# Attention two units at a time over one ring of score banks, and two weight tiles loaded later in the experts

## The chip, the cores and the metric

One Trainium2 chip, one core. The metric is the device time of one execution in microseconds (us), taken as the median of the runs shown. The engines are named as the profile names them: PE (TensorE matmul), PEld (its weight load), DVE (VectorE), ACT (ScalarE), POOL (GpSimd), SP (SyncE, which here only issues DMAs).

## The reference, cut to what matters

```python
def reference(**kwargs):
    attn_out = _attn_ref(q, k, v, n_global=8, n_local=96)   # 2 x 8 heads x 768 x 64
    x = attn_out.transpose(0, 2, 1, 3).reshape(B, S, H * D) # 2 x 768 x 512
    x = _moe_ref(x, w_gate, w_local, w1, w2)                # 8 experts, one per token
    return _moe2_ref(x, w_theta, w_tok_r, w_tok_i, w_ch)

# attention: banded + first keys, a linear bias per head, softmax, times v
scores = q @ k.T / sqrt(64) + bias;  scores = where(keep, scores, -1e9)
a = exp(scores - max) / (sum + 1e-9);  attn_out = a @ v
# experts: per token one expert e (a sequential choice), p[e] * (relu(x @ w1[e]) @ w2[e])
# last part: theta = x @ w_theta; y = w_tok_r @ (x cos theta) + w_tok_i @ (x sin theta)
#            u = x + y; out = u + relu(u @ w_ch)
```

## The kernel before, in words

Everything is float32 at the interface. Where precision allows no single pass, an operand is split into a high and a low part and three products are taken. The program is written out in Python; each engine takes its instructions in the order in which the program issues them, and semaphores are set by the framework, which also guards PSUM by whole banks. So the order of the calls is the schedule.

There are three stages: attention with the routing of tokens to experts, the experts, and the last part (theta, token mixing, channel product).

**Attention.** A unit is one block of 128 queries of one batch and one pair of heads: 12 blocks (`BLOCKS`, alternating over the two batches) times 4 pairs, 48 units. The blocks 0 and 1 see 128 keys, the others 256 (the last 96 before the block, the first 32, the block's own 128). A unit goes through these steps:

- `u_qk` (L572): scores, PE. Each of the two heads uses 64 rows of the array (L583, three products of high and low parts: 6 matmuls, two at a time side by side; L587 for the first two blocks).
- `u_soft` (L592), once per head: DVE adds the bias and takes the minimum (L605), ACT takes the exponential with its sum (L615).
- `u_tr` (L631): 4 full-array transposes on PE (L638); `u_cp` (L641): ACT copies them from PSUM to SBUF (L647; for a few early units DVE, L645).
- `u_pv` (L650): times v, 8 matmuls on PE with 64 output columns each (L662), two at a time side by side.

When the 4 units of a block are done, `blk_evac` (ACT, L674), `blk_rinv`, the logits (`lg`, `lc`, `lt`, `ld`: L223, L227, L230, L235), `blk_tr` (L679) and `blk_store` (L688, DMA `xd<-xt`) follow, and for every two blocks ten routing stages (`ch` to `tk`).

The loop `for step in range(TAIL0)` (L899) takes one unit per step: scores of unit `step`, some warm-up matmuls in the first 12 steps, v-product of unit `step-6`, softmax of unit `step-1`, a high/low split of a coming block's q or k (cast on ACT or DVE, rest on POOL), the late block and routing stages that are due in this step (a dictionary `later`), then transposes and copy of unit `step-4`. From unit 40 on the order is the hand-written string `TAIL`; it ends with a first expert tile computed ahead (`lead_*`: a gather of 128 rows, L750, and `lead_h`, `lead_y`).

PSUM in this stage: `pS` (scores: two buffers for each head, `s0` and `s1`), `pT` (2 buffers, shared by the transposes of probabilities, the transposed block `y`, the logits and the slot table), `pX` (v-product), `pM` (routing rows and warm-up).

**Experts.** Eight experts in order of size, each in 8 steps of 128 hidden columns, so `for u in range(64)` (L1524). Weights come in 512 KB pieces of two steps: `load_piece(n, (1,))` for w1 (ring of 3) and `(n, (2,))` for w2 (ring of 5), issued by SP in program order. The first ones are issued before the loop: piece 0 of w1, then the list `LOADS`. In step u: `mm1(u+2)` (L1404), `mm2(u)` (L1443, L1454), the split of w1 for u+3 (`split_w1`: ACT L1268, DVE L1269; a finished pair triggers the next w1 load), the split of w2 for u+1 (`split_w2`: ACT L1371, DVE L1372), `relu(u+2)`. In steps 2 and 3 ACT issues the first two loads of the matrices of the last part (`job_load`, L390, `jraw`); a background job (`job`, L395) works on them in between, first with an ACT instruction on the loaded data (L407). In step 1 two small stores of the token probabilities (`pd`, L1554) are issued.

**Last part.** Starts when the experts' rows are stored; its bulk is the token mixing on PE (L1712).

Of the kernel before, what the change touches and what calls it, by code (L numbers as in the profile page):

```python
# [9 lines left out]
F32 = mybir.dt.float32  # L10
# [7 lines left out]
PSUM = bass.MemoryType.PSUM  # L18
# [3 lines left out]
E, DM, FF = 8, 512, 1024  # L22
# [37 lines left out]
TAIL = """  # L60
pv34 yt7 sa39 tr36 cp36 ys7 qk40 pv35 ro3 sb39 tr37 ev8 sc3 cp37 sa40 tr38 cp38 qk41 sb40 oh3 ho3 pv36 lg8
sa41 lc8 sb41 qs11 fi ri8 pv37 po3 fi tr39 qk42 ks11 cp39 pv38 ri9 pl3 pv39 ev9 mk3 sa42 sb42 lt8 yt8 ld8 fi
# [19 lines left out]
W0, W1 = 8, 0  # L82
LOADS = ((1, 1), (0, 2), (2, 1), (1, 2), (2, 2), (3, 2), (4, 2))
PU = 1
# [18 lines left out]
def kernel(  # L103
# [339 lines left out]
    with ExitStack() as actx:  # L443
        ab = actx.enter_context(tc.tile_pool(name="ab", bufs=3, side="right"))
        ap = actx.enter_context(tc.tile_pool(name="ap", bufs=3, side="right"))
        pS = actx.enter_context(tc.tile_pool(name="pS", bufs=2, space=PSUM))
        pT = actx.enter_context(tc.tile_pool(name="pT", bufs=2, space=PSUM))
# [114 lines left out]

        SPLITS = {3: lambda: split_q(2), 4: lambda: split_k(2), 8: lambda: split_k(1)}

        WARM = dict.fromkeys(range(12), WPS) | {3: 6} | dict.fromkeys(range(4, 9), 2)

# [4 lines left out]

        def u_qk(u):  # L572
            n, j = units[u]
            sp = [pS.tile([128, 256], F32, tag=f"s{hh}", name=f"s{hh}") for hh in range(2)]
            cols = slice(j * 128, (j + 1) * 128)
            half = [slice(64 * hh, 64 * hh + 64) for hh in range(2)]
            b, t = divmod(n, NT)
            if t:
                kh, kl = [x[:, b, j, t * 160 - 96 : t * 160 + 160] for x in kparts]
                qh, ql = [w[:, BLOCKS.index(n) % 4, cols] for w in qparts]  # L580
                for i, (qa, ka) in enumerate(((qh, kh), (ql, kh), (qh, kl))):
                    for hh in range(2):
                        PE.matmul(sp[hh], lhsT=qa[half[hh]], rhs=ka[half[hh]], start=(i == 0), stop=(i == 2))  # L583
            else:
                q, k = packs[n]
                for hh in range(2):
                    PE.matmul(  # L587
                        sp[hh][:, 0:128], lhsT=q[half[hh], j], rhs=k[half[hh], j, 32:160], start=True, stop=True
                    )
            ust[u] = {"s": sp}  # L590

        def u_soft(u, hh):  # L592
            n, j = units[u]
            W = 256 if n % NT else 128
            bias = bias1 if n % NT else bias0
            if hh == 0:
                ust[u]["t"] = (
                    ap.tile([128, 2, 256], F32, tag="sm", name="sm"),
                    ap.tile([128, 2, 256], F32, tag="pr", name="pr", bufs=5),
                    ap.tile([128, 2], F32, tag="st", name="st", bufs=4),  # L600
                )
# [74 lines left out]
        def blk_tr(n):  # L676
            yp = yps[n] = pT.tile([128, 512], F32, tag="pt", name="y")
            for j in range(4):
                PE.transpose(yp[:, j * 128 : (j + 1) * 128], xTs[n][:, j], ident)  # L679
# [17 lines left out]
        def mps(own):  # L697
            return (pM if own else pT).tile([128, 512], F32, tag="m" if own else "pt", name="m")

# [42 lines left out]
        def lead_x():  # L742
# [5 lines left out]
            V.tensor_copy(head_i, idf)  # L748
            x = head["x"] = ap.tile([128, 2, 256], F32, tag="sm", name="x0")
            G.indirect_dma_start(  # L750
# [21 lines left out]
        def lead_tr():  # L772
            x = head["x"].rearrange("p a c -> p (a c)")
            tp = head["xp"] = pS.tile([128, 4, 128], F32, tag="s0", name="x0T")
            for j in range(4):
                PE.transpose(tp[:, j], x[:, j * 128 : (j + 1) * 128], ident)

        def lead_cp():
            xT = ap.tile([128, 2, 256], F32, tag="sm", name="x0T")
            head["xT"] = xT.rearrange("p a (b c) -> p (a b) c", b=2)  # L780
            A.activation(head["xT"], head.pop("xp"), AF.Copy)
            head["h"], head["hs"] = {}, {}

        def lead_h(f, c):
            if c == 0:
                head["h"][f] = pS.tile([128, 128], F32, tag="s1", name="h0")
            w = head["w"][f][:, 0].rearrange("p (a f) -> p a f", a=4)
            for j in (2 * c, 2 * c + 1):
                PE.matmul(head["h"][f], lhsT=w[:, j], rhs=head["xT"][:, j], start=(j == 0), stop=(j == 3))  # L789

        def lead_r(f):
            if f % 4 == 0:
                h = ap.tile([128, 2, 256], F32, tag="sm", name="h0")
                head["hs"][f // 4] = h.rearrange("p a (b c) -> p (a b) c", b=2)
            A.activation(head["hs"][f // 4][:, f % 4], head["h"].pop(f), AF.Relu)

        def lead_y(f, c):
            if f == 0 and c == 0:
                head["y"] = pS.tile([128, DM], F32, tag="s0", name="y0")
            o = slice(c * 256, (c + 1) * 256)  # L800
# [63 lines left out]

        later, pairs = {}, {}

# [31 lines left out]

        for step in range(TAIL0):  # L899
            n, j = units[step]  # L900
            i = step // 4 + 2
            if j == 0 and step and i < NB:
                load_qk(i)
                load_v(i)
            u_qk(step)
            warm(WARM.get(step, 0))
            u = step - 1
            if u == 2:
                mask1()
            if 0 <= u < 4:  # L910
                biases(0, u)
            if 5 <= u < 9:
                biases(1, u - 5)
            done = None
            if step >= 6:
                u_pv(step - 6)
                if units[step - 6][1] == 3:
                    done = units[step - 6][0]
            if u >= 0:
                u_soft(u, 0)  # L920
            if done is not None:
                blk_evac(done)
            if u >= 0:
                u_soft(u, 1)
            i = step // 4 + 1
            if step in SPLITS:
                SPLITS[step]()
            elif 2 < i < NB and step % 4 == 1:
                split_q(i)
            elif 2 < i < NB and step % 4 == 2:  # L930
                split_k(i)
            if done is not None:
                blk_rinv(done)
                st = blk_done(done)
                for lag, names in ((1, ("lg", "lc")), (2, ("lt", "ld"))):
                    for k in names:
                        after(step + lag, st[k])
                if done >= NT:
                    st = pairs[done % NT] = pair_stages(done % NT)
                    for lag, names in ((2, ("ch",)), (3, ("ro", "sc")), (4, ("oh", "ho")), (5, ("po", "pl", "mk")), (8, ("sl", "tk"))):  # L940
                        for k in names:
                            after(step + lag, st[k])
                after(step + 3, partial(blk_tr, done))
                after(step + 3, partial(blk_store, done))
            for fn in later.pop(step, []):
                fn()
            if step >= 4:
                u_tr(step - 4)
                u_cp(step - 4)
            if step == 20:  # L950
                scalars()
                window_flag()
            if step >= 16 and step % 2:
                fill()
        assert all(s < TAIL0 for s in later) or True

        ops = {}
        for u in range(NU):
# [5 lines left out]
            ops[f"pv{u}"] = partial(u_pv, u)  # L964
        blks = {}

# [325 lines left out]
    with ExitStack() as mctx:  # L1292
# [231 lines left out]
        for u in range(64):  # L1524
# [10 lines left out]
            if u in (2, 3):  # L1535
                job_load()
            mm1(u + 2)
            mm2(u)
# [422 lines left out]
```

## Time and profile before

| | us |
|---|---|
| median of 3 runs | 514.17 (513.6 to 516.56) |
| the profiled execution | 510.26 |
| its span, first to last instruction | 508.5 |
| PE busy in the span | 481.8 |
| DVE, ACT, POOL busy | 352.0, 267.6, 146.4 |

The span is cut into 40 slices of 12.7 us; a digit is the busy share of an engine in a slice in tenths. Attention takes the first 8 slices (to about 104 us), the work ahead on the first expert tile the next two, the experts follow up to two thirds of the row, and the last part is the rest. Busy time is a union: two matmuls side by side count once. The clock that PE was granted stands beside it in tenths of full speed.

### The profile page before, as it was taken

The page shows a single profiled execution, that of the slowest core. Times are in us where ns is not written, and L with a number is a line of the kernel's source. Part 1 is how long each engine was busy: PE and PEld are TensorE (multiplying, and loading weights), DVE is VectorE, ACT ScalarE, POOL GpSimd, SP SyncE. Part 2 cuts the span into 40 slices and gives each one's busy share as a digit, 9 for nine tenths or more (in the row PEclk, how much of TensorE's full clock was granted, in tenths as well). Part 3 has the DMA queues.
Part 4 walks back from the last instruction along what each step waited for, and adds up shares of the span by engine and source line. Part 5 has one row for each costly group of instructions (what it writes and reads, how often), then busy time and mean ns, then how long its engine had stood idle before and what let it go on. Part 6 is the DMA issues. An engine that isn't in the chain of part 4 may idle for free.

```text
span 508.5 us, 9738 instructions
## 1 busy us (share of the span) xinstructions
PE 481.8 (95%) x3416; PEld 393.2 (77%) x3417; DVE 352.0 (69%) x963; ACT 267.6 (53%) x647; POOL 146.4 (29%) x164
## 2 busy tenths in 40 slices
PE   8999999979849999999999989989999999999996
PEld 4577777658738889878888777868888888888886
DVE  6887777935637688876788989547787787571522
ACT  5787888651425566655556556446556365340300
POOL 6445753323203230302122011111534244250300
PEclk9999999999988999999999999999999999999999
DMA  8557565377977698777799984320132000000022
GB/s 282 166 150 233 175 219 190 144 246 246 306 191 241 190 334 294 238 249 245 232 321 340 339 295 163 131 105 0 36 112 62 22 21 22 0 1 31 32 105 83
DMA packets 53253, 86.34 MB, mean 170 GB/s; under 512 B 6512, under 2 KB 28784, under 8 KB 53200
## 3 DMA queue, kind: packets, MB, share of 16 engines
q1 hardware_dynamic: 44644, 64.82, 38.9%
q10 hardware_dynamic: 5804, 13.93, 8.2%
q0 software_dynamic: 2752, 6.93, 4.6%
q8 instruction: 28, 0.46, 0.4%
q14 instruction: 25, 0.20, 0.2%
HBM read 71.17 MB, written 14.49 MB: 168 GB/s over the span
## 4 chain that ended last, share of the span: by engine, by line
PE 72%; DMA 11%; DVE 9%; issue 3%; ACT 2%; POOL 1%; ACTq 0%; DVEq 0%; POOLq 0%
PE a L1712 20%; PE o L1443 7%; PE b L1749 7%; PE th L1636 6%; PE h L1404 6%; PE x L662 4%; DMA raw<-in_w_dram 4%; PE h L1388 4%; PE pt L638 3%; PE s L583 3%; DMA jraw<-in_w_tokT_dram 2%; DVE w2s L1372 2%; PE o L1454 2%; DMA jraw<-in_w_theta_dram 2%; PE h L789 2%
## 5 line engine op out<-in xcount | busy, mean ns | idle before, releaser
L1712 PE MATMUL a<-wtok,z 128*128 128x512 f32 x576 | 105.3, 341 | 0.0
L1712 PEld LDWEIGHTS a<-wtok,z 128*128 128x128 f32 x576 | 88.5, 188 | 13.1 <-ACT z L1687 0.3
L1443 PE MATMUL o<-w2s,hh 128*128 128x512 f32 x192 | 66.4, 421 | 2.8 <-DVE w2s L1372 1.6
L1404 PE MATMUL h<-xT,w1s 128*128 128x288 f32 (+3 forms) x384 | 54.7, 290 | 10.1 <-ACT w1s L1268 7.2
L1404 PEld LDWEIGHTS h<-xT,w1s 128*128 128x128 f32 x384 | 50.5, 193 | 14.4 <-ACT w1s L1268 7.9
L615 ACT ACTIVATE pr<-sm,st 128x256 f32<-128x256 f32 (+1 forms) x96 | 46.1, 483 | 11.6 <-DVE st L605 11.6
L1372 DVE TENSOR_TENSOR w2s<-raw,w2s 128x512 fp32r<-128x512 f32 x64 | 44.0, 688 | 5.3 <-ACT w2s L1371 2.7
L1388 PE MATMUL h<-xT,raw 128*128 128x192 f32 (+1 forms) x256 | 44.4, 316 | 1.0 <-issue 0.9
L1036 POOL DMA_INDIRECT xg<-xd,xidx x17 | 16.8, 990 | 96.8 <-PE tr L1243 90.9
L1388 PEld LDWEIGHTS h<-xT,raw 128*128 128x128 f32 x256 | 39.6, 189 | 5.2 <-issue 3.2
L1371 ACT ACTIVATE w2s<-raw 128x512 fp32r<-128x512 f32 x64 | 39.8, 623 | 4.3 <-DMA raw<-in_w_dram 2.0
L1443 PEld LDWEIGHTS o<-w2s,hh 128*128 128x128 f32 x192 | 33.0, 188 | 9.5 <-DVE w2s L1372 4.4
L1418 ACT ACTIVATE hh<-h 128x128 fp32r<-128x128 f32 (+3 forms) x64 | 20.4, 319 | 34.6 <-PE h L1404 18.8
L1443 PE MATMUL o<-w2s,hl 128*128 128x512 f32 x96 | 38.1, 397 | 0.0
L605 DVE CUSTOM_DVE_ANT_0 sm<-s,bias 128x256 f32<-128x256 f32 (+1 forms) x96 | 34.3, 392 | 0.2
L1668 POOL TENSOR_TENSOR si<-si,yg 128x512 f32<-128x512 f32 x10 | 13.4, 1344 | 60.7 <-ACT si L1661 51.4
L662 PE MATMUL x<-ps,vv 128*64 128x128 f32 x352 | 29.4, 286 | 0.3 <-ACT xT L674 0.2
L647 ACT ACTIVATE ps<-pt 128x512 f32<-128x512 f32 (+1 forms) x44 | 24.9, 567 | 8.1 <-PE pt L638 7.7
L638 PE MATMUL pt<-ident,pr 128*128 128x128 f32 x176 | 28.4, 281 | 0.4 <-ACT pr L615 0.3
L1757 DVE SCALAR_TENSOR_TENSOR ob<-b,xTf 128x512 f32<-128x512 f32 (+1 forms) x16 | 8.8, 557 | 27.6 <-PE b L1749 27.6
L1269 DVE TENSOR_TENSOR w1s<-raw,w1s 128x512 fp32r<-128x512 f32 x32 | 22.1, 689 | 8.1 <-ACT w1s L1268 7.4
L583 PE MATMUL s<-wtok,qp 64*128 64x256 f32 x240 | 25.2, 313 | 0.1
(264 smaller groups left out, 951.3 us busy)
## 6 DMA issues: line engine op xcount, KB each, us to landing
raw<-in_w_dram SPq DMA_DIRECT2D x64, 512.0 KB
qk<-in_pack_dram SPq DMA_DIRECT2D x11, 576.0 KB
jraw<-in_w_tokT_dram ACTq DMA_DIRECT2D x11, 512.0 KB
vv<-in_pack_dram SPq DMA_DIRECT2D x10, 512.0 KB
w<-in_w_dram SPq DMA_DIRECT2D x16, 256.0 KB
yd<-zero SPq DMA_DIRECT2D x13, 256.0 KB
xd<-xt SPq DMA_DIRECT2D x12, 256.0 KB
jraw<-in_w_tokT_dram ACTq DMA_DIRECT2D x10, 256.0 KB
```

The costliest lines, as they stand in the source:

```text
L583: PE.matmul(sp[hh], lhsT=qa[half[hh]], rhs=ka[half[hh]], start=(i == 0), stop=(i == 2))
L605: V.tensor_tensor_reduce(out=sm[:, hh, 0:W], in0=ust[u]["s"][hh][:, 0:W], in1=bias[:, 2 * j + hh], scale=-0.125, scalar=BIG, op0=ALU.add, ...
L615: A.activation(pr[:, hh, 0:W], sm[:, hh, 0:W], AF.Exp, bias=st[:, hh : hh + 1], scale=-1.0, accum_out=sums[n][:, 2 * j + hh : 2 * j + hh + 1],
L638: PE.transpose(pt[:, hh, c], pr[:, hh, c * 128 : (c + 1) * 128], ident)
L662: PE.matmul(xp[64 * hh : 64 * hh + 64, j], lhsT=vv[:, i, h * 64 : (h + 1) * 64], rhs=ps[:, hh, c], start=(c == 0), stop=(c == nch - 1),)
L1371: A.activation(h2, bb[:, o], AF.Copy)
L1372: V.tensor_tensor(l2, bb[:, o], f32(h2), op=ALU.subtract)
L1388: PE.matmul(hp[:, :N], lhsT=pieces[u // 2][1][:, j, o * 128 : (o + 1) * 128], rhs=x[:, j, :N], start=(j == 0), stop=(j == 3),)
L1404: PE.matmul(hp[:, :N], lhsT=wa[:, j], rhs=xa[:, j, :N], start=(k == 0), stop=(k == 11))
L1443: PE.matmul(out[:M], lhsT=ha[:, lo : lo + M], rhs=wa, start=(f == 0 and q == 0), stop=(f == 7 and q == 2),)
L1712: PE.matmul(acc[b][d][o], lhsT=za[:, d * 128 : (d + 1) * 128], rhs=wa[:, c, lo:hi], start=(t == 0 and n == 0 and (o == 0 or d % 2 == 0)), ...
L1749: PE.matmul(op[:, : hi - lo], lhsT=wa[:, d, e * 128 : (e + 1) * 128], rhs=ua[:, d, lo:hi], start=(n == 0), stop=(n == 11),)
```

## The change

Two independent parts.

First, the attention loop takes two units per step (`p`), `a = 2p` and `b = 2p+1`. Their scores share banks: one `[128, 512]` bank per head, unit a in columns 0 to 255, unit b in 256 to 511. `pS` becomes one ring of 4 banks (tag `s`), from which the transposed block `y`, the logits and the slot table also take a bank each (before: from `pT`); in the tail each unit takes two banks of this ring. The result of the first expert tile moves from `pS` to `pX`. Softmax of a pair follows its scores in the same step. Three SBUF rings grow by one buffer. The warm-up matmuls are dealt out anew (25 in place of 22), the splits of blocks 1 and 2 sit in steps 1 to 3 of the pairs, and the first line of `TAIL` is adapted.

Second, the w2 pieces 3 and 4 leave `LOADS` and are issued in steps 1 and 3 of the experts.

```diff
-LOADS = ((1, 1), (0, 2), (2, 1), (1, 2), (2, 2), (3, 2), (4, 2))
+LOADS = ((1, 1), (0, 2), (2, 1), (1, 2), (2, 2))
...
-        pS = actx.enter_context(tc.tile_pool(name="pS", bufs=2, space=PSUM))
+        pS = actx.enter_context(tc.tile_pool(name="pS", bufs=4, space=PSUM))
...
-        SPLITS = {3: lambda: split_q(2), 4: lambda: split_k(2), 8: lambda: split_k(1)}
-        WARM = dict.fromkeys(range(12), WPS) | {3: 6} | dict.fromkeys(range(4, 9), 2)
+        SPLITS = {1: lambda: split_q(2), 2: lambda: split_k(2), 3: lambda: split_k(1)}
+        WARM = dict(enumerate((2, 8, 6, 4, 3, 2)))
...
-        def u_qk(u):
+        def u_qk(u, with_last=False):
             n, j = units[u]
-            sp = [pS.tile([128, 256], F32, tag=f"s{hh}", name=f"s{hh}") for hh in range(2)]
+            if with_last:
+                sp = [x[:, 256:512] for x in ust[u - 1]["banks"]]
+            else:
+                banks = [pS.tile([128, 512], F32, tag="s", name=f"s{hh}") for hh in range(2)]
+                sp = [x[:, 0:256] for x in banks]
...
         def blk_tr(n):
-            yp = yps[n] = pT.tile([128, 512], F32, tag="pt", name="y")
+            yp = yps[n] = pS.tile([128, 512], F32, tag="s", name="y")
...
         def mps(own):
-            return (pM if own else pT).tile([128, 512], F32, tag="m" if own else "pt", name="m")
+            return (pM if own else pS).tile([128, 512], F32, tag="m" if own else "s", name="m")
...
-        for step in range(TAIL0):
...
+        for p in range(TAIL0 // 2):
+            a, b = 2 * p, 2 * p + 1
+            i = a // 4 + 2
+            if a % 4 == 0 and p and i < NB:
+                load_qk(i)
+                load_v(i)
+            u_qk(a)
+            u_qk(b, True)
+            warm(WARM.get(p, 0))
+            i = a // 4 + 1
+            if p in SPLITS:
+                SPLITS[p]()
+            elif 2 < i < NB:
+                (split_q if p % 2 else split_k)(i)
...
+            u_soft(a, 0)
+            u_soft(b, 0)
+            full_mode(p)
+            if p >= 2:
+                u_tr(a - 4)
+                u_cp(a - 4)
+                u_tr(b - 4)
+            u_soft(a, 1)
+            u_soft(b, 1)
+            if p >= 2:
+                u_cp(b - 4)
+            for fn in early.pop(p, []):
+                fn()
+            if p >= 3:
+                u_pv(a - 6)
+                u_pv(b - 6)
+                n, j = units[b - 6]
+                if j == 3:
+                    blk_evac(n)
+                    blk_rinv(n)
...
             if u in (2, 3):
                 job_load()
+            if u in (1, 3):
+                load_piece(3 + u // 2, (2,))
```

`full_mode(p)` runs the late block and routing stages that are due in step p (`lt`, `ld`, `yt`, `ys`, `ch` to `tk`); `early` holds the logits (`lg`, `lc`) of a block that was finished one step before.

## Rows read from the trace of the kernel before

**Rows 1.** The page: span, and PE busy in 40 slices (tenths).
```profile
span 508.5 us, 9738 instructions
...
PE   8999999979849999999999989989999999999996
```

**Rows 2.** Busy time by stretch; columns as the first line names them.
```profile
core 0: us, PE busy (x) PEld busy (x) DVE busy (x) ACT busy (x) POOL busy (x), PEclk, DMA share, GB/s
...
16.00:24.00 8.00, 7.95 (x70) 4.38 (x69) 7.64 (x29) 5.95 (x24) 4.36 (x3) 1.00 0.53 164
24.00:82.00 58.00, 57.85 (x633) 42.39 (x633) 44.85 (x220) 48.17 (x155) 30.89 (x30) 1.00 0.62 194
82.00:104.00 22.00, 20.75 (x240) 15.48 (x236) 19.42 (x95) 15.48 (x46) 7.22 (x10) 1.00 0.40 145
...
144.00:151.50 7.50, 0.25 (x2) 0.06 (x1) 0.51 (x2) 1.29 (x3) 0.00 (x0) 0.86 0.67 117
151.50:156.50 5.00, 4.88 (x16) 4.23 (x17) 4.97 (x11) 2.10 (x5) 0.00 (x0) 0.52 0.67 181
```

**Rows 3.** PE in order of time: start, us, what, count; one step of the loop.
```profile
62.43 0.66 PE L638 MATMUL pt<-ident,pr 128*128 128x128 f32 x4
63.02 0.62 PE L583 MATMUL s<-wtok,qp 64*128 64x256 f32 x6
63.57 0.66 PE L662 MATMUL x<-ps,vv 128*64 128x128 f32 x8
64.16 0.33 PE L230 MATMUL m<-ident,lT 128*128 128x128 f32 x1
```

**Rows 4.** PE in order of time, where two units' work stands together.
```profile
84.53 1.09 PE L638 MATMUL pt<-ident,pr 128*128 128x128 f32 x8
85.55 0.62 PE L583 MATMUL s<-wtok,qp 64*128 64x256 f32 x6
...
103.56 1.09 PE L662 MATMUL x<-ps,vv 128*64 128x128 f32 x16
104.59 0.33 PE L230 MATMUL m<-ident,lT 128*128 128x128 f32 x1
```

**Rows 5.** Line L583 from 24 to 82 us: matmul duration, least, median, most (ns).
```profile
L583 PE MATMUL s<-wtok,qp x164: 271/277/387, 23.9 to 80.1; 64*128 64x256 f32 x164
```

**Rows 6.** Chain of waits from 5 to 24 us: start, us, what.
```profile
22.31 1.57 POOL wtok L498
...
23.93 0.38 PE s L583
```

**Rows 7.** All engines in order of time in the tail; idle time before in brackets.
```profile
90.85 0.62 PE L583 MATMUL s<-wtok,qp 64*128 64x256 f32 x6
...
92.11 0.23 DVE L235 TENSOR_TENSOR lh<-m,sums 128x72 f32<-128x72 f32 x1
...
92.48 0.43 PE L223 MATMUL m<-xT,wg 128*32 128x128 f32 x8 [1.01 <-ACT pr L615]
```

**Rows 8.** Chain of waits over the whole span: two loads for the background job.
```profile
141.83 8.35 DMA jraw<-in_w_theta_dram
...
285.79 4.30 DMA jraw<-in_w_tokT_dram
```

**Rows 9.** PE in order of time at the start of the experts.
```profile
143.81 0.39 PE L1443 MATMUL o<-w2s,hl 128*128 128x512 f32 x1
151.44 3.73 PE L1404 MATMUL h<-xT,w1s 128*128 128x288 f32 x12 [7.25 <-ACT w1s L1268]
```

**Rows 10.** SP's queue: the loads of expert weights, merged.
```profile
129.38 4.44 SPq L1024 DMA_DIRECT2D raw<-in_w_dram  x4
134.07 3.51 SPq L1020 DMA_DIRECT2D raw<-in_w_dram  x2
```

**Rows 11.** DMA queues from 142 to 150 us (q1 is SP's, q10 ACT's).
```profile
q1 hardware_dynamic: 2540, 0.99, 48.8%
q10 hardware_dynamic: 144, 0.52, 16.9%
```

More of the change, by code (lines that the diff above doesn't have):

```diff
@@ L60 @@
 TAIL = """
-pv34 yt7 sa39 tr36 cp36 ys7 qk40 pv35 ro3 sb39 tr37 ev8 sc3 cp37 sa40 tr38 cp38 qk41 sb40 oh3 ho3 pv36 lg8
+pv34 lt7 ld7 yt7 tr36 cp36 ys7 sl2 tk2 ch3 qk40 pv35 ro3 tr37 ev8 sc3 cp37 sa40 tr38 cp38 qk41 sb40 oh3 ho3 pv36 lg8
 sa41 lc8 sb41 qs11 fi ri8 pv37 po3 fi tr39 qk42 ks11 cp39 pv38 ri9 pl3 pv39 ev9 mk3 sa42 sb42 lt8 yt8 ld8 fi
@@ L590, in u_qk @@
             ust[u] = {"s": sp}
+            if not with_last:
+                ust[u]["banks"] = banks
         def u_soft(u, hh):
@@ L597, in u_soft @@
                 ust[u]["t"] = (
-                    ap.tile([128, 2, 256], F32, tag="sm", name="sm"),
-                    ap.tile([128, 2, 256], F32, tag="pr", name="pr", bufs=5),
-                    ap.tile([128, 2], F32, tag="st", name="st", bufs=4),
+                    ap.tile([128, 2, 256], F32, tag="sm", name="sm", bufs=4),
+                    ap.tile([128, 2, 256], F32, tag="pr", name="pr", bufs=6),
+                    ap.tile([128, 2], F32, tag="st", name="st", bufs=5),
                 )
@@ L748, in lead_x @@
             V.tensor_copy(head_i, idf)
-            x = head["x"] = ap.tile([128, 2, 256], F32, tag="sm", name="x0")
+            x = head["x"] = ap.tile([128, 2, 256], F32, tag="sm", name="x0", bufs=4)
             G.indirect_dma_start(
@@ L773, in lead_tr @@
             x = head["x"].rearrange("p a c -> p (a c)")
-            tp = head["xp"] = pS.tile([128, 4, 128], F32, tag="s0", name="x0T")
+            tp = head["xp"] = pS.tile([128, 512], F32, tag="s", name="x0T").rearrange("p (j c) -> p j c", j=4)
             for j in range(4):
@@ L778, in lead_cp @@
         def lead_cp():
-            xT = ap.tile([128, 2, 256], F32, tag="sm", name="x0T")
+            xT = ap.tile([128, 2, 256], F32, tag="sm", name="x0T", bufs=4)
             head["xT"] = xT.rearrange("p a (b c) -> p (a b) c", b=2)
@@ L785, in lead_h @@
             if c == 0:
-                head["h"][f] = pS.tile([128, 128], F32, tag="s1", name="h0")
+                head["h"][f] = pS.tile([128, 512], F32, tag="s", name="h0")[:, 0:128]
             w = head["w"][f][:, 0].rearrange("p (a f) -> p a f", a=4)
@@ L792, in lead_r @@
             if f % 4 == 0:
-                h = ap.tile([128, 2, 256], F32, tag="sm", name="h0")
+                h = ap.tile([128, 2, 256], F32, tag="sm", name="h0", bufs=4)
                 head["hs"][f // 4] = h.rearrange("p a (b c) -> p (a b) c", b=2)
@@ L798, in lead_y @@
             if f == 0 and c == 0:
-                head["y"] = pS.tile([128, DM], F32, tag="s0", name="y0")
+                head["y"] = pX.tile([128, 4, 128], F32, tag="x", name="y0").rearrange("p j c -> p (j c)")
             o = slice(c * 256, (c + 1) * 256)
@@ L863, in experts_slots @@
             V.scalar_tensor_tensor(yidx, slotf[:, 0], 128.0, slotf[:, 1], op0=ALU.add, op1=ALU.add)
-        later, pairs = {}, {}
+        later, early, pairs = {}, {}, {}
         def after(step, fn):
@@ L897, in pair_stages, with full_mode @@
             return dict(zip(("ch", "ro", "sc", "oh", "ho", "po", "pl", "mk", "sl", "tk"), route_stages(t, mps, msb)))
-        for step in range(TAIL0):
-            n, j = units[step]
-            i = step // 4 + 2
-            if j == 0 and step and i < NB:
+        blks = {}
+        def full_mode(p):
+            for fn in later.pop(p, []):
+                fn()
[3 more added lines that the diff above has]
+            if a % 4 == 0 and p and i < NB:
@@ L903 @@
                 load_qk(i)
                 load_v(i)
[L905 to L944, printed above, removed]
@@ L945 @@
-            for fn in later.pop(step, []):
-                fn()
[L947 to L950, printed above, removed]
+            u_qk(a)
[6 more added lines that the diff above has]
+                (split_q if p % 2 else split_k)(i)
+            if p < 4:
+                t = p // 2
+                if p == 1:
+                    mask1()
+                for k in (2 * (p % 2), 2 * (p % 2) + 1):
+                    biases(t, k)
@@ new lines @@
+            u_soft(a, 0)
[10 more added lines that the diff above has]
+            for fn in early.pop(p, []):
+                fn()
+            if p >= 3:
[5 more added lines that the diff above has]
+                    blk_rinv(n)
+                    st = blks[n] = blk_done(n)
+                    early.setdefault(p + 1, []).extend(st[k] for k in ("lg", "lc"))
+                    after(p + 2, st["lt"])
+                    after(p + 2, st["ld"])
+                    after(p + 2, partial(blk_tr, n))
+                    after(p + 2, partial(blk_store, n))
+                    if n >= NT:
+                        st = pairs[n % NT] = pair_stages(n % NT)
+                        for lag, names in ((2, ("ch",)), (3, ("ro", "sc")), (4, ("oh", "ho")), (5, ("po", "pl", "mk")), (6, ("sl", "tk"))):
+                            for k in names:
+                                after(p + lag, st[k])
@@ L951 @@
+            if p == 10:
                 scalars()
                 window_flag()
-            if step >= 16 and step % 2:
+            if p >= 8:
                 fill()
-        assert all(s < TAIL0 for s in later) or True
         ops = {}
@@ L964 @@
             ops[f"pv{u}"] = partial(u_pv, u)
-        blks = {}
         def blk_op(i, k):
```

## The prediction

> **What bounds the kernel now.** I read the page's slices first: PE is at nine tenths in nearly every slice of a span of 508.5 us, with one hole of two slices [rows 1]. Then busy time by stretch. In the attention loop, 24 to 82 us, PE is busy 57.85 of 58 us while DVE has 44.85 and ACT 48.17; so PE is the bound there and the others have room. In the stretch before it DVE has 7.64 of 8 us, and in the tail, 82 to 104, DVE has 19.42 of 22: there DVE is as near to the bound as PE. From 144 to 151.5 PE does next to nothing, and afterwards its clock is granted at 0.52 for 5 us [rows 2].
>
> Busy is not the same as well used, so third the order of time on PE. One step of the loop: transposes start at 62.43, scores at 63.02, the v-product at 63.57, the next full-array work at 64.16. That is 0.59, 0.55 and 0.59 us, 1.73 us per unit [rows 3]. Where two units' transposes happen to stand together, eight take 1.02 us from 84.53 to the next kind, not 2 x 0.59; sixteen v-products take 1.03 us from 103.56 [rows 4]. So four more transposes cost 0.43 us and eight more v-matmuls 0.44: what is paid once per group, and not per matmul, is 0.16 and 0.15 us, the change from one shape of the array to another. Scores show the same inside a group: six matmuls in pairs take 0.62 us [rows 3] of which the last lasts 0.28 (the median), the first up to 0.39 [rows 5].
>
> Last the chain of waits. At the start of the experts ACT issues a background load at 141.83 that lands 8.35 us later [rows 8]; the split of w1 is queued behind its first use on ACT, and PE stands 7.25 us for it [rows 9].
>
> **The loop, 14 pairs (units 12 to 39).** It removes every second change of shape and adds no matmul. Per pair now 2 x 1.73 = 3.46 us. After: transposes 1.02, v-product 1.03 [rows 4], scores 0.55 plus three more pairs of matmuls. A further pair costs 0.11 us if it goes as the others do (0.43 / 4 and 0.44 / 4); from rows 3 and 5 alone it is at most (0.62 - 0.28) / 2 = 0.17. That gives 0.88 (at most 1.06), together 2.93 (3.11), a gain of 0.53 (0.35) per pair and of 7.4 us (4.9). I take the first, as it rests on two runs of the kind itself. The change from v-product straight to scores is not in the trace; either way I allow 0.1 us for it, 1.4 us in all.
>
> What hides the rest: block and routing stages are the same instructions as before. PE would need 57.85 / 14 - 0.53 = 3.60 us per pair, ACT has 48.17 / 14 = 3.44, DVE 44.85 / 14 = 3.20 [rows 2]. PE stays the bound, but ACT's cover shrinks from 0.69 to 0.16 us per pair, and order now matters. Two places where I see PE wait: in a step with a slot table the ring of four banks gives `y` the bank that `ld` on DVE must first read, about 0.5 us, twice in the loop; and ACT comes late at the second transposes' copy after an evacuation, some 0.4 us in sum. I give back 1.4 us: loop -6.0. If ACT became the bound outright it would still be 3.44 per pair; lost cover of 0.35 per pair is rival B.
>
> **The start, units 0 to 11.** DVE is nearly full (0.36 us idle in 16 to 24 [rows 2]), and the last wait before unit 12 is a split on POOL that ends at 23.88, just before its scores at 23.93 [rows 6]. The splits come one place earlier, three warm-ups are added on a PE that waits here anyway. I take -0.4, DVE's idle time. At best the split of 1.57 us leaves the path, -1.6; at worst the same on the other side, since the split of block 2's q now stands in front of four exponentials on ACT and waits there for its load: +1.6.
>
> **The tail.** The order stays, but scores, `y`, logits and the slot table share four banks. Counting allocations through the string, scores of unit 43 now need the bank that `ld8` reads; this read starts on DVE at 92.11, the scores went at 90.85. Before, PE stood 1.01 us at the logits right after that [rows 7], so this wait mostly takes that one's place; but units 44 and 45 and `y9` then each find a bank whose reader is one or two DVE instructions behind. About 0.7 us. The two waits of unit 47 lie beside the wait for a gather. Bounds 0, if DVE is that much earlier, and +2.5. If this part were serial it would be rival D.
>
> **The experts.** SP's bytes are the same, two loads move. Of the four w2 loads merged at 129.38 two leave; the two w1 loads at 134.07 [rows 10] move up. Piece 3 follows in step 1, behind the w1 load that waits for step 0, so before the background load at 141.83 again; piece 4 goes in step 3, behind ACT's split of step 2, so after it. From 142 to 150 SP's queue moves 0.99 MB and ACT's 0.52 [rows 11]: one piece of 0.52 MB less stands beside the background load. The least that such a load takes on the chain is 4.30 us [rows 8]; if the other 4.05 us are due to the 0.99 MB, 0.52 of them are worth 2.1 us. I take -2.1. Bounds 0 (it has its own 0.52 MB and two small stores beside it) and -4.05. ACT, SP and DVE issue nothing more than before; piece 4 is needed in step 7, some four steps after its issue. The granted clock has a mean of 0.86 over these 7.5 us [rows 2]: of its two levels, 2.4 and 1.2 GHz, that is the lower one for the last 2.1 us, so it fell some 5.2 us after the last matmul. A wait of 7.25 - 2.1 = 5.15 us lies right beside that; I take that it falls again, 0, and -2.3 if it does not (4.88 us of PE work at about half speed [rows 2]).
>
> **Sum.** -0.4 - 6.0 + 0.7 - 2.1 = -7.8 us. From 144 us on each stage waits for its own predecessors, so I carry it to the end whole. The profiled execution took 510.26 us, 3.91 below the median of 514.17; against the median the forecast is 506.4.
>
> **Rivals.**
> A, the forecast, 506.4.
>
> B, the shared bank: unit a's softmax may start only when unit b's scores are in the same bank, three pairs of matmuls later, 0.33 us. For it: ACT and DVE now start each pair behind PE, and before each head had a bank of its own. Against it: DVE's 3.20 us of 3.60. If all of it lies on the path, 14 x 0.33 = 4.6 us go: -3.2, 511.0. The Trainium skill, "PSUM — Partial Sum Buffer", section on bank collisions, has it as a rule that speaks against this change: guard PSUM "by **bank × quadrant** (by bank is the simple version), not by address"; no run here shows a read of one half while the other is written.
>
> C, the stall at 144 us goes further: the load lands as the fastest does, -4.05, and the clock stays, -2.3: -0.4 - 6.0 + 0.7 - 4.05 - 2.3 = -12.1, 502.1. For it: the DMA traffic there is what differs. Against: the load's own bytes, and a pause of 3 us remains.
>
> D, slower: scores of a pair wait for the last softmax of the pair before, through the ring. Then PE and DVE alternate: 0.88 + 0.28 + 3.20 = 4.36 us per pair against 57.85 / 14 = 4.13, +3.2; and in the tail, eight units, 0.55 + 0.28 + 19.42 / 8 = 3.26 each against 22 / 8 = 2.75, +4.1. With the start and the experts as above: -0.4 + 3.2 + 4.1 - 2.1 = +4.8, 519.0. It decides from the point where the bank that a pair's second head gets was last read by an instruction at the end of DVE's queue for the pair before. By my count of the ring that is so only in the two steps after a slot table, and in the tail for units 43, 44 and 47.
>
> E, the change does not do what it says: the time between groups is not the change of shape but a wait for the operands. Then the loop gives nothing: -1.8, 512.4. Against: rows 4 show the same operands' kinds without it.
>
> **Chances.** A 0.52, B 0.17, C 0.17, D 0.07, E 0.07. A measurement of this kernel tells about 0.5%, 2.6 us, from no change, so faster means under 511.6. A is that but for a fiftieth, C surely, B half: 0.76 faster. E, half of B and the rest of A: 0.17 the same. D: 0.07. The range from 500.5 (C with a good start) to 513.0 (E with a poor one) leaves out D and a little of either end.
>
> **What will show it.** In the changed profile: groups of 8 transposes, 12 scores, 16 v-products in the loop, the 12 scores in 0.88 us to the next kind, and the step for two units near 3.7 us; PE still full from 24 to about 76 us (if DVE or ACT ends its waits, B or D). Scores of unit 43 in the tail held by DVE. The background load landing some 6 us after its issue and PE's wait near 5 us, with the clock at half after it. I am wrong if the loop ends less than 3 us earlier, or if the tail grows by more than it gained.

## The result, and the profile after

The changed kernel took 508.06 us in the median of 4 runs, the kernel before 513.88: ratio 0.9871, 95% interval 0.9825 to 0.9918. The forecast was 506.4, range 500.5 to 513. The profiled execution took 507.36 us, before 510.26. On other chips the kernel before ran from 506.9 to 519.7 us; where the change ran again (e5), its median was 515.75 beside 513.46, and as five of its six runs lie over 1.5% above the sixth (505.83) and count as slow, there is no second ratio. Much of this spread goes with the clock: in a fit to the 125 runs that the comparisons use, with a level for each kernel, time falls 4.2 us per 0.01 of mean granted clock. At one clock the change stands 3.8 +- 1.8 us below before, its attention part alone (e1) 1.8 +- 1.4 below, its loads alone (e2) 0.3 +- 1.1 above (+- is two standard errors of the fit). With all 162 runs whose clock is on record in the fit, ten of them of the change, the change stands 1.8 +- 1.3 below. So a gain of 1.3% was not seen a second time.

So the total came out near the forecast. Its terms did not. The profile after, span and PE slices, to hold against [rows 1]:

```profile
span 505.6 us, 9746 instructions
...
PE   8888998989969999999999989899999999999996
```

Busy time by stretch, with the columns and four of the stretches of [rows 2]:

```profile
16.00:24.00 8.00, 7.79 (x78) 5.41 (x75) 5.18 (x24) 6.46 (x28) 4.13 (x4) 0.84 0.57 185
24.00:82.00 58.00, 51.64 (x617) 40.83 (x617) 43.22 (x215) 46.01 (x155) 29.81 (x30) 1.00 0.61 197
82.00:104.00 22.00, 20.82 (x225) 15.60 (x227) 18.59 (x89) 13.62 (x40) 6.66 (x9) 1.00 0.36 134
144.00:151.50 7.50, 3.47 (x13) 3.26 (x14) 4.21 (x9) 3.05 (x7) 0.00 (x0) 0.78 0.71 33
```

PE was full in the loop before, 57.85 of 58 us; now it does its work in fewer busy microseconds, 51.64, and stands for 6.4. The saving in array changes is there, and almost all of it has become waiting. The waits from 24 to 76 us (engine, line, whom it waited for: us in total, times, longest):

```profile
ACT pr L622 <- DVE xt L695: 12.0, 7, 2.1
...
DVE sm L612 <- PE s L588: 8.8, 7, 1.6
...
PE m L230 <- ACT lT L227: 2.1, 5, 0.7
...
PE pt L645 <- ACT ps L654: 1.7, 5, 0.4
...
PE m L334 <- POOL ohl L325: 0.9, 2, 0.7
```

Of ACT's waits in the kernel before, the same stretch, none is for `xt`:

```profile
ACT pr L615 <- DVE st L605: 5.0, 8, 1.1
ACT ps L647 <- PE pt L638: 4.0, 11, 0.6
```

One pair of the changed loop, all engines in order of time (start, us, engine, line, what; idle time before in brackets):

```profile
63.84 0.98 PE L588 MATMUL s<-wtok,qp 64*128 64x256 f32 x12
...
64.96 0.42 DVE L612 CUSTOM_DVE_ANT_0 sm<-s,bias 128x256 f32<-128x256 f32 x1 [1.55 <-PE s L588]
...
65.80 0.66 PE L686 MATMUL y<-ident,xT 128*128 128x128 f32 x4
...
66.29 1.04 PE L645 MATMUL pt<-ident,pr 128*128 128x128 f32 x8
66.49 0.69 DVE L695 TENSOR_TENSOR xt<-y,sums 128x512 f32<-128x512 f32 x1
...
67.21 0.51 ACT L622 ACTIVATE pr<-sm,st 128x256 f32<-128x256 f32 x1 [1.82 <-DVE xt L695]
67.25 1.09 PE L669 MATMUL x<-ps,vv 128*64 128x128 f32 x16
...
68.28 0.39 PE L588 MATMUL s<-wtok,qp 64*128 64x256 f32 x2
```

The groups are as forecast: 8 transposes in 0.96 us to the next kind, 16 v-products in 1.03, 12 scores in 0.91. But ACT's exponential of unit a starts at 67.21, although its input was ready when the softmax of 64.96 ended. It waits for a multiply into `xt` of another block. The pair takes 4.44 us.

At the experts, the chain of waits over the whole span, after and then before:

```profile
140.32 6.11 DMA jraw<-in_w_theta_dram
148.43 3.01 PE h L1417 x11
...
321.30 1.71 PE th L1819 x12
323.06 5.71 DMA yg<-yd,yidx
329.80 3.40 PE a L1727 x12
```

```profile
152.17 3.01 PE h L1404 x11
...
325.72 1.71 PE th L1804 x12
327.47 5.32 DMA yg<-yd,yidx
333.55 2.32 PE a L1712 x12
```

The background load lands 6.11 us after its issue, 8.35 before [rows 8]; PE resumes 3.74 us earlier (148.43 for 152.17) and is 4.42 us ahead at the first `th`. There 1.5 us are lost again: the gather takes 0.39 us longer, and after it the twelve matmuls take 3.40 us for 2.32, at a granted clock of 0.68 from 330 to 334 us (1.00 in before), so for part of that time at the lower of its two levels.

All runs in one table; "12 to 40" is from the scores of unit 12 to those of unit 40, the 14 pairs of the prediction's loop term (53.8 us forecast); "landing" is the first background load from issue to landing, and the last column is the part of it behind the last packet of this load.

| | what | ratio to before | 12 to 40, us | landing, us | behind the last packet, us |
|---|---|---|---|---|---|
| before | | 1 | 59.82 | 8.35 | 2.3 |
| after | the change | 0.9871 [0.9825, 0.9918] | 60.64 | 6.11 | 1.3 |
| e1 | attention part alone | 0.9978 [0.993, 1.0026] | 60.62 | 9.02 | 2.5 |
| e2 | loads alone | 1.0038 [0.9994, 1.0083] | 59.83 | 9.73 | 4.2 |
| e3 | after, softmaxes ahead of stages | 1.0205 [1.0145, 1.0265] | 64.86 | 8.63 | 1.8 |
| e4 | after, own banks | 1.0187 [1.0131, 1.0243] | 67.34 | 8.50 | 3.8 |
| e5 | the change again | none | 60.64 | 9.55 | 5.2 |
| e6 | after, four `sums` | 0.9949 [0.9902, 0.9996] | 59.18 | 9.08 | 3.6 |
| e7 | e6 and new order | 0.9844 [0.9768, 0.9919] | 55.73 | 7.92 | 3.7 |
| e8 | before again | none (one run) | 59.49 | 8.38 | 2.7 |
| e9 | e7, token stage later | 0.9879 [0.9828, 0.9929] | 55.78 | 8.33 | 3.9 |
| e10 | e9, probabilities later | 0.9855 [0.9806, 0.9905] | 55.76 | 5.23 | 0.5 |
| e11 | e9, own banks | 1.0064 [1.003, 1.0098] | 62.98 | 8.01 | 3.3 |
| e12 | e10, slot stage later | 0.982 [0.9762, 0.9878] | 53.36 | 6.11 | 0.5 |

### The profile page after: what moved, and what is told of

Same layout as the page of the kernel before. It is cut to its first block, busy times and chain, and to the rows that moved or that the text cites. A ratio compares the mean times of both kernels' runs of the same rounds, so it can differ in the third digit from the quotient of the medians.

```text
span 505.6 us, 9746 instructions
## 1 busy us (share of the span) xinstructions
PE 475.6 (94%) x3418; PEld 394.3 (78%) x3420; DVE 347.9 (69%) x963; ACT 265.5 (53%) x647; POOL 145.8 (29%) x164
## 4 chain that ended last, share of the span: by engine, by line
PE 57%; DMA 8%; DVE 4%; ACT 2%; issue 1%; ACTq 1%; DVEq 0%
PE a L1727 20%; PE o L1456 9%; PE h L1417 8%; PE b L1764 7%; PE th L1651 6%; DMA jraw<-in_w_tokT_dram 4%; PE h L1401 4%; PE o L1467 2%; DMA yd<-yo 1%; DMA jraw<-in_w_theta_dram 1%; DMA yg<-yd,yidx 1%; PE b L1615 1%; DVE w2s L1385 1%; PE tr L1256 1%; DVE jw L412 1%
## 5 line engine op out<-in xcount | busy, mean ns | idle before, releaser
L1727 PE MATMUL a<-wtok,z 128*128 128x512 f32 x576 | 106.5, 344 | 0.0
L1727 PEld LDWEIGHTS a<-wtok,z 128*128 128x128 f32 x576 | 89.7, 190 | 13.1
L645 PE MATMUL pt<-ident,pr 128*128 128x128 f32 x176 | 26.4, 280 | 4.5 <-ACT ps L654 4.0
L669 PE MATMUL x<-ps,vv 128*64 128x128 f32 x352 | 26.0, 284 | 0.0
L645 PEld LDWEIGHTS pt<-ident,pr 128*128 128x128 f32 x176 | 19.3, 140 | 8.5 <-ACT ps L654 5.9
```

The lines of the kernel that those rows point to most:

```text
L645: PE.transpose(pt[:, hh, c], pr[:, hh, c * 128 : (c + 1) * 128], ident)
L669: PE.matmul(xp[64 * hh : 64 * hh + 64, j], lhsT=vv[:, i, h * 64 : (h + 1) * 64], rhs=ps[:, hh, c], start=(c == 0), stop=(c == nch - 1),)
L1727: PE.matmul(acc[b][d][o], lhsT=za[:, d * 128 : (d + 1) * 128], rhs=wa[:, c, lo:hi], start=(t == 0 and n == 0 and (o == 0 or d % 2 == 0)), ...
```

## The experiments

**e1 and e2: the two parts apart.**

```diff
 # e1, against after
-LOADS = ((1, 1), (0, 2), (2, 1), (1, 2), (2, 2))
+LOADS = ((1, 1), (0, 2), (2, 1), (1, 2), (2, 2), (3, 2), (4, 2))
-            if u in (1, 3):
-                load_piece(3 + u // 2, (2,))
 # e2, against before: the same lines the other way
```

> The changed kernel with the old order of the experts' loads and without the two early loads: the attention part alone. Theory 1 (the loop gained almost nothing, the experts' loads nearly all): the two traces stand 0.3 us apart at the first matmul of the experts, 130.85 against 131.14, so this kernel stands at 0.998 to 1.000 of the kernel before, the first landing of the background load takes about 8.3 us again and TensorE waits over 6 us at 145. Rival (the loop gave more than this one trace shows, since the medians differ by 6 us and the traces by 2.9): 0.993 to 0.996, with the first experts' matmul 2 to 3 us earlier than 131.1.

> The kernel before with the new order of the experts' loads and the two early loads: the experts' part alone. Theory 1: landing 6 us after its issue, TensorE resumes about 3.7 us earlier at 148, and most of it is kept to the end: 0.990 to 0.994 of the kernel before (-3 to -5 us). Rival: the gain at 148 is given back at a later load, as 1.5 us were at the last gather in the trace of after; then 0.996 to 0.999.

Neither part reaches 0.5%. The loops are those of after and before to 0.02 us (60.62 and 59.83). The load is what surprises: with the new order it lands latest of all,

```profile
142.69 9.73 DMA jraw<-in_w_theta_dram
```

and with the old order after 9.02 us. Theory 1 is right about the loop and wrong about the loads: what the first trace gained at 148 us does not come back with the loads alone.

**e3: the softmaxes ahead of the stages.**

```diff
             u_soft(a, 0)
             u_soft(b, 0)
+            u_soft(a, 1)
+            u_soft(b, 1)
             full_mode(p)
...
-            u_soft(a, 1)
-            u_soft(b, 1)
```

> The changed kernel with all four softmaxes of a pair put ahead of the block's stages on VectorE and ScalarE; TensorE's order is the same. Theory A (the loop is held by a ring of waits: TensorE waits for ScalarE's copies, ScalarE for the second softmaxes, and these stand on VectorE behind the multiply that waits for TensorE's y; ScalarE's 12 us of idle time by that multiply in 24 to 76): a pair takes 3.7 to 3.9 us instead of 4.12, unit 38 starts at 71.5 to 74 instead of 76.5, time 0.990 to 0.996 of after (-2 to -5 us). Rival B (the bank shared by both units: VectorE starts on unit a only when unit b's scores are written, 0.45 us late): no change of the pair, 4.1 us, 0.999 to 1.001 of after. Rival C (stages that come later hold the copies or the routing more): 4.2 us or more per pair, over 1.001 of after.

2% slower than the kernel before, and its loop 4.2 us longer than that of after: against theory A. Its waits from 24 to 76 us:

```profile
ACT pr L622 <- DVE xt L695: 14.0, 6, 2.6
...
PE pt L645 <- ACT ps L654: 6.8, 6, 1.7
```

ACT still waits for `xt`, and longer, although the second softmaxes no longer stand behind it. The wait stands once per block, at the first exponential of its first unit (7 from 24 to 76 us in after), and the only thing that this instruction shares with a multiply into `xt` is `sums`: it writes its row sums into a new `sums` buffer, of which there are three, and the multiply is the last to read the one of three blocks earlier. In before the multiply of block m comes in step 4m + 12 and the first softmax of block m + 3 in step 4m + 13: in front of it on DVE. In the new loop both fall into pair 2m + 6, and the softmax is first.

**e4: own banks for each unit.**

```diff
-            if with_last:
-                sp = [x[:, 256:512] for x in ust[u - 1]["banks"]]
-            else:
-                banks = [pS.tile([128, 512], F32, tag="s", name=f"s{hh}") for hh in range(2)]
-                sp = [x[:, 0:256] for x in banks]
+            banks = [pS.tile([128, 512], F32, tag="s", name=f"s{hh}") for hh in range(2)]
+            sp = [x[:, 0:256] for x in banks]
```

> The changed kernel with two banks of its own for each unit of a pair, in the same ring of four, so that a unit's softmax waits for its own scores alone; y and the stages' tiles still come from the ring. Theory A: VectorE starts on unit a 0.4 us earlier, but the second softmaxes still wait behind the stages, so a pair takes 4.1 us or more, as scores can now wait for the ring; 0.998 to 1.006 of after. Rival B: 3.8 us or less per pair, unit 38 at 73 or before, 0.992 to 0.996 of after.

The loop is 6.7 us longer; it does not speak for rival B, but with ACT standing still it does not settle it either (e11).

**e5 and e8: the change and the kernel before once more**, without an edit.

> The changed kernel once more, beside the kernel before on this chip, where the attention part alone measured 0.998 and the loads alone 1.004. Theory 1 (the two parts add, each near nothing, and the 1.3 per cent of the first comparison were mostly what single runs vary by): 0.995 to 1.003 of before. Rival (the two parts help each other): 0.985 to 0.992. The loop of this run is as in the first trace: unit 38 at 76.5, ScalarE idle 12 us in 24 to 76 by VectorE's multiply into xt.

> The kernel before, a second trace, for the landing of the background load and the wait at 145 under the old loads. Theory 1 (the load lands sooner with the new loads): 8 to 9 us from issue to landing and 20.5 to 21 us from the first matmul of the experts to the one after the wait, against under 18 in the trace of after. Rival (the landing differs from run to run whatever the loads): anything from 6 to 10 us, with runs of the new loads spread over the same range.

e5's loop is that of the first trace (60.64 both times); its median, 515.75 beside 513.46, speaks for theory 1, though without a ratio it does not decide. e8's loop is 0.33 us shorter than that of the first trace of before. The landing: old loads 8.35, 8.38, 9.02; new loads, up to e7, 6.11, 7.92, 8.50, 8.63, 9.08, 9.55, 9.73. The spread of the new lies around the old: the order of the loads does not set it. On the transfer itself the loads may act: from the issue to its last packet the load took 5.7, 6.0 and 6.5 us with the old loads and 4.2 to 6.9, in the median 4.8, in the eleven traces with the new (5.5 in e2). No run tests this apart, and what comes behind the last packet covers it (e10).

**e6: one more buffer of `sums`.**

```diff
-                    sums[n] = ap.tile([128, 8], F32, tag="sums", name="sums")
+                    sums[n] = ap.tile([128, 8], F32, tag="sums", name="sums", bufs=4)
```

> The changed kernel with four buffers of sums instead of three. Theory D (the first softmax of each block writes its row sums into the buffer of three blocks earlier, whose last reader is the multiply into xt; the change put that multiply behind it in VectorE's order, so ScalarE stands still once per block, 7 times 1.6 to 2.1 us in 24 to 76; this also explains why putting the stages later made it worse): the 12 us of idle time are gone, TensorE's waits for ScalarE's copies fall from 5 us to under 2, unit 38 starts at 72 to 74.5 instead of 76.5, and the time is 0.992 to 0.997 of the changed kernel's. Theory A (the second softmaxes stand behind the stages on VectorE): ScalarE then waits at the second softmaxes instead, unit 38 at 75.5 or later, 0.998 to 1.000. Rival B (bank shared by both units): no change, 1.000.

The cause is hit: ACT's waits for `xt` are gone; what is left of ACT's, from 21 to 76 us, is

```profile
ACT pr L622 <- DVE st L612: 4.6, 10, 0.9
ACT ps L654 <- PE pt L645: 3.4, 4, 2.0
```

The gain is smaller than theory D had it: 1.5 us in units 12 to 40, unit 38 at 74.58. Part of the rest is one event. Up to 46.47 PE waited 1.12 us for GpSimd's one-hot (`ohl`, L325, which the slot stage's matmul reads), and its clock fell; stretches around it:

```profile
43.00:46.50 3.50, 2.19 (x34) 1.73 (x31) 2.61 (x12) 3.40 (x12) 3.16 (x4) 1.00 0.97 336
46.50:49.00 2.50, 2.50 (x19) 2.45 (x20) 1.91 (x9) 0.46 (x3) 1.43 (x1) 0.64 0.40 151
49.00:51.00 2.00, 2.00 (x19) 1.53 (x17) 1.64 (x10) 1.57 (x6) 0.12 (x1) 0.60 0.00 0
```

At 0.64 and 0.60 these 4.5 us hold about 1.7 us less work. In the times no step shows: at one clock e6 stands 3.5 +- 1.3 us below before, the change 3.8 +- 1.8.

**e7: four `sums`, and transposes, copies, softmaxes, stages in this order.**

```diff
             u_soft(a, 0)
             u_soft(b, 0)
-            full_mode(p)
             if p >= 2:
                 u_tr(a - 4)
-                u_cp(a - 4)
                 u_tr(b - 4)
+                u_cp(a - 4)
+                u_cp(b - 4)
             u_soft(a, 1)
             u_soft(b, 1)
-            if p >= 2:
-                u_cp(b - 4)
+            full_mode(p)
...
+  (ps: bufs=4)
```

> Four buffers of sums and four of ps, and in each pair TensorE's transposes, then ScalarE's copies, all four softmaxes and only then the block's stages. Theory D with A as the second cause: a pair takes 3.65 to 3.8 us, the forecast's 3.7, unit 38 at 70.5 to 73, 0.988 to 0.995 of the changed kernel. Theory D alone: the same as with four buffers of sums, within 0.5 us at unit 38. Rival C (the block's routing comes late for the tail): unit 38 early, but the first matmul of the experts no earlier than 130.

Ratio 0.9844, a pair takes 3.80 us, unit 38 starts at 70.81: as D with A as the second cause had it. The order and the fourth buffer of `ps` came together and were not tried apart, nor was the new order with three buffers of `sums`. PE's waits left, 24 to 76 us:

```profile
PE m L334 <- POOL ohl L325: 1.9, 2, 1.1
PE m L230 <- ACT lT L227: 0.9, 1, 0.9
```

**e9: the token stage a pair later.**

```diff
-... (5, ("po", "pl", "mk")), (6, ("sl", "tk"))):
+... (5, ("po", "pl", "mk")), (6, ("sl",)), (7, ("tk",))):
```

> The kernel of e7 (four buffers of sums and of ps, softmaxes ahead of the stages) with the token stage's matmuls one pair later than the slot stage. Theory E (in e7 TensorE waits 1.1 us in the pairs of units 24 and 32 for GpSimd's second 416 wide one-hot, as both stages stand in one pair): these two pairs take 4.0 us or less instead of 5.3 and 4.9, unit 38 at 68.5 to 69.8 instead of 70.8, time 2 us less than e7's at the same clock. Rival (another wait takes its place, as ScalarE's or VectorE's queue is full): unit 38 at 70.3 or later, same time as e7.

A miss. Units 24 and 32 take 5.27 and 4.87 us as in e7, because the matmul that waits is still there:

```profile
44.66 0.18 PE L334 MATMUL m<-rbm,ohl 128*128 128x16 bf16 x1
45.97 0.42 PE L334 MATMUL m<-rbm,ohl 128*128 128x16 bf16 x7 [1.12 <-POOL ohl L325]
```

L334 is the slot stage, `sl`; `tk` has only DVE's additions. The stage that I moved was the wrong one (e12). The change itself had moved it: from mask to slot stage three units lie in before (5 and 8 steps), one pair in the change (5 and 6).

**e10: the probabilities' stores a unit later.**

```diff
             if u == PU:
                 probs()
+            if u == PU + 1:
                 for b in range(B):
                     SP.dma_start(pd...[b], ptok[...])
```

> The kernel of e9 with the two stores of the tokens' probabilities (768 packets of 4 bytes) one unit later, so that they are issued behind the wait for the background load instead of beside it. Theory F (its landing, 6.1 to 9.7 us after the issue and 0.8 to 3.7 us after the last packet, is held by these packets and not by the order of the experts' loads): landing 5 to 6.5 us, TensorE's wait 4 to 5 us instead of 6 to 8, end 2 to 3 us earlier than e9 at the same clock. Rival G (the landing is held by the large loads ahead of it, as the prediction had it): landing and wait as in the other runs, 7.9 to 9.7 and 6 to 8 us; time as e9 within 0.5 us.

Theory F holds for the landing, not for the end. e9's chain, then e10's:

```profile
140.25 8.33 DMA jraw<-in_w_theta_dram
```

```profile
139.81 5.23 DMA jraw<-in_w_theta_dram
```

The data arrives at the same time in both: the load's last packet ends at 144.65 us in e9 and 144.57 in e10, and then it is 3.93 us to the landing in the one and 0.47 in the other. In e9 the queues from 144.7 to 148.5 hold nothing but the tail of the two stores (packets, bytes, share of 16 engines):

```profile
DMA packets 186, 0.00 MB, mean 0 GB/s; under 512 B 186, under 2 KB 186, under 8 KB 186
...
q1 hardware_dynamic: 186, 0.00, 2.8%
```

All traces of the table agree: in the twelve with the two stores beside the load 1.3 to 5.2 us pass from its last packet to the landing, with hardly anything but packets of 4 bytes on the queues, and 0.5 in the two without them (e10, e12). The expectation's 0.8 to 3.7 us is too low. PE in order of time, e9 and then e10:

```profile
149.86 3.73 PE L1416 MATMUL h<-xT,w1s 128*128 128x288 f32 x12 [7.61 <-ACT w1s L1280]
```

```profile
146.30 0.40 PE L1416 MATMUL h<-xT,w1s 128*128 128x288 f32 x1 [3.28 <-ACT w1s L1280]
```

PE's hole, from one start to the next, falls from 8.0 to 3.7 us and the first `th` comes 2.2 us earlier. The end does not: 0.3 us later, since the last gather takes 6.80 us in place of 5.50 and the clock after it is low (0.62 from 330 to 334 us), as in after. The times (0.9879 and 0.9855) can't tell the two apart.

The Trainium skill, "DMA: Bandwidth & Descriptors", section on queues, rings and completion order, has the rule behind this: a transfer's completion write lands only after every earlier write of the same DMA engine, across its queues. These runs agree, with 3.93 against 0.47 us.

**e11: own banks in the new order**, the edit of e4 on e9.

> The kernel of e9 with two banks of its own for each unit of a pair. Rival B (the shared bank costs 0.3 us a pair, since VectorE starts on unit a only when unit b's scores are written): unit 38 3 us or more earlier than in e9. Theory D and A (the shared bank is covered once ScalarE no longer stands still): unit 38 as in e9 or later, since the ring of four banks now has to wait for the softmaxes of the pair before; 0 to 5 us longer than e9.

Rival B falls. Unit 38 starts at 78.70, in e9 at 70.96: 7.7 us later, more than the 0 to 5 us expected. PE now waits for the ring, 24 to 76 us:

```profile
PE s L585 <- DVE st L607: 5.0, 8, 0.9
```

**e12: the slot stage later too, on e10.**

```diff
-... (6, ("sl",)), (7, ("tk",))):
+... (7, ("sl", "tk"))):
```

> The kernel of e10 with the slot stage moved one pair later as well: in e9 only the token stage (VectorE alone) was moved, and the matmul that waits for GpSimd's one-hot is the slot stage's, so the two long pairs stayed. Theory E as corrected: the pairs of units 24 and 32 take 4.1 us or less instead of 5.27 and 4.87, unit 38 at 68.5 to 69.5 instead of 70.9, and with theory F the landing 5 to 6.5 us after its issue; 0.980 to 0.986 of before. Rival: the wait for the one-hot moves to another pair, unit 38 at 70.3 or later, 0.985 to 0.990.

504.22 us median against 514.37, ratio 0.982; at one clock 9.2 +- 1.7 us below before. It beats both kernels. The loop, 24 to 68 us, and PE's only wait from 24 to 76:

```profile
24.00:68.00 44.00, 43.98 (x548) 36.42 (x546) 39.22 (x196) 39.87 (x133) 25.09 (x26) 1.00 0.70 224
```

```profile
PE m L230 <- ACT lT L227: 0.9, 1, 0.9
```

PE is full again to 68 us. Units 12 to 38 take 46.96 us, 3.61 per pair, and 54.30 in before: 0.56 us per pair saved, where the prediction had 0.53.

## Why the prediction was right and wrong

*The price of an array change* was right: 0.53 us per pair forecast, 0.56 in e12, with the groups' lengths as forecast. Rival E falls. The sum that follows has a slip: 1.4 us are set aside twice, for the change from v-product to scores (14 times 0.1) and for two waits (twice 0.5 and 0.4), and -7.4 to -6.0 takes in only one of them; with both it is -4.6. The first was hardly needed: the v-products take 1.03 us up to the scores, as forecast, and the scores 0.91 for 0.88.

*The loop, -6.0 us,* is the step that failed. From unit 12 to 40 the change took 60.64 us, 0.82 longer than before. Unit 40 starts at 83.50 for 83.19, so the prediction's own sign of being wrong, a loop that ends less than 3 us earlier, is met. The failing term is "I give back 1.4 us": the step came out 6.8 us above its 53.8, the whole saving gone into waits. The prediction counted through the rings of banks and named two waits, of which ACT's late copies showed (1.7 us for its 0.4) and the bank of `y` did not. It did not look at what the block's store, put two pairs later, frees. That was a buffer of `sums`, 32 bytes a partition; through it ACT stood 12.0 us, its copies and `lT` came late, and PE waited for those. With ACT's cover at 0.16 us per pair, as the prediction had worked out itself, a wait of 1.7 us every second pair could not be hidden. e6, e7 and e12, each built on the one before, give it back: 1.5, 4.9 and 7.3 us of units 12 to 40 in all. So the buffer of `sums` alone is the smaller part, 1.5 us; order and `ps` add 3.4, the slot stage's earlier place another 2.4. How much of e6's small share is due to the clock event there and how much to the order stays open. The last pair, 38 to 40, is a loss of its own: 7.03 us for 5.52, with the stages that were moved to the head of the tail's string.

*Rivals B and D.* B's mechanism is there: DVE starts on unit a at 64.96, when the scores of unit b, too, are written (the last of them start at 64.55). The rule that the prediction quotes from the Trainium skill's "PSUM — Partial Sum Buffer" (section on bank collisions: guard by bank) agrees with this start. The shared bank has no price left in e12, where PE is busy 43.98 of 44 us; own banks cost 7.2 us in units 12 to 40 (e11 against e9). D's alternation of PE and DVE is what the waits look like (DVE 8.8 us behind scores), but its cause isn't the ring.

*The start, -0.4,* was -0.51 in the first trace (unit 12 at 22.86 for 23.37) with the clock at 0.84 from 16 to 24 us; at full clock unit 12 starts at 21.60 in the same kernel (e5) and at 21.25 in e1, -1.8 and -2.1, beyond the bound of -1.6.

*The tail, +0.7:* units 40 to 47 took 20.24 us for 19.47, +0.77, and the place is right: unit 43's scores wait 0.92 us for DVE. In e5, with the clock at 0.88 from 90 to 104 us (1.00 here), the same units took 21.44.

```profile
92.28 0.96 PE L588 MATMUL s<-wtok,qp 64*128 64x256 f32 x6 [0.92 <-DVE st L612]
```

*The experts, -2.1.* The landing (6.11) came out as forecast, PE's wait at 4.21 us for 5.15, and the clock fell again, as taken (0.78 from 144 to 151.5 us); the reason holds in part at most. The prediction named the "two small stores beside it" only as what might leave nothing to gain; they hold the end of the landing (e10), by 2.3 us in before and 1.3 in after. Of the 2.24 us between these two landings 1.27 lie ahead of the last packet, where 0.52 MB less of large loads could act, and 0.97 behind it. The loads alone (e2) landed at 9.73 and gained no time. That the first trace landed early is within what runs of one kernel differ by (6.11 in after, 9.55 in e5).

*Carried whole to the end:* no. Of 4.42 us at the first `th` 2.86 are left at the last matmul; the gather of `yg` and the clock after it take the rest.

So the total was near by luck. Two errors had opposite signs in the traces compared: the loop gave nothing, and the experts gave more than the change had put there. Even so these two executions differ by 2.9 us only (510.26 and 507.36); the other half of the 5.8 between the medians is what single runs vary by.

## What to carry to other kernels

When a change moves a reader later in program order, list every buffer that it is the last to read, the smallest too, and count who reuses it: a ring of three that was just long enough stalls the engine that writes the fourth. Before shortening the bounding engine's work, compare its new time with the next engines' (here 3.60 against 3.44 us): with a cover of 0.16 us each wait that was hidden comes to light, and order and buffers have to be set anew for the gain to appear. If a load is late, look at when its last packet ended; if the data is there and the signal is not, look for small stores on the same engines.

## What the runs showed of the hardware that was not expected

A load's completion came 3.93 us after its last packet beside two stores of 768 packets of 4 bytes each, and 0.47 us without them (e9, e10; 0.48 in e12); over the twelve traces with these stores it was 1.3 to 5.2 us.

The same wait of 1.1 us for GpSimd was followed by a lower granted clock in e6 (0.64 and 0.60 for 4.5 us) and by no fall in e7 and e9, where the granted clock was 1.00 from 24 to 76 us. What tells these apart stays open.

Single runs of one kernel differ by 2.5% with their mean granted clock (0.974 to 0.993 for before), more than the change is worth; the length of the loop in the traces of one loop repeats to 0.05 us, but for e8 (0.33), and told the parts apart where the times could not.
